# U's product in the low-rank mixer: six matmuls of 256 columns for two batches, twelve of 128 columns for the other two

## The chip, the cores and the metric

The kernel runs on one core of one Trainium2 chip. The metric is the device time of one execution in microseconds; the lower the better. The core has five engines that run beside each other, each with a queue of its own: TensorE (PE: matmuls, and PEld, the loads of their stationary operand), VectorE (DVE), ScalarE (ACT), GpSimd (POOL) and SyncE (SP, which issues the transfers here). Transfers run on 16 DMA engines.

## The reference

Two layers follow each other: a state-space layer (Mamba-2 in chunks) over 4 batches, 8 heads and 768 tokens, and a mixer with a low-rank product over the tokens and a two-layer network over the channels.

```
# state-space layer, per batch and head, in chunks of 32 tokens
M = (C @ B.T) * L;  y = M @ x + (C @ state) * decay;  state = decay * state + B.T @ x
# bridge: (B, H, S, D) -> x of (4, 768, 256)
xt = x.transpose(0, 2, 1)                 # (4, 256, 768)
h = xt @ U @ V                            # U (768, 32), V (32, 768)
u = x + h.transpose(0, 2, 1)
ch = np.maximum(u @ w_ch1, 0.0) @ w_ch2   # 256 -> 1024 -> 256
return u + ch
```

What the change touches is `xt @ U`: for each batch, 768 tokens are summed into 32 ranks for each of 256 channels.

## The kernel before

Tokens are taken in 6 blocks of 128 a batch (`NC`), channels in 2 halves of 128 (`NCB`). The state-space layer goes through 12 pairs of blocks, `k` = 0 to 11, three to a batch; its products are small ones in parts of the array: `gram` (L510), `state` (L545), `inter` (L630), `intra` (L655). `yout` copies its result to `yT` (channels by tokens) on ACT, and `ytokening` turns that on PE (L682) to `ytok` (tokens by channels). The transposes at L478 turn B and C.

The mixer of batch `b` follows. `project` is U's product (L712): the stationary operand is a block of U (128 tokens by 32 ranks), the moving operand the tokens of `ytok`, and the result goes into one of four quadrants of 32 partitions of one PSUM bank "w", so that each quadrant holds a part of the sum over the tokens. ACT copies the bank to `pT` (L717). `parted` adds the four quadrants with one product with a constant matrix (`spot`, L722) and copies the sum to `ps` (L724, and L725 on DVE). `added` multiplies by V (L732) and adds onto `yT` on DVE. The wide products of the two-layer network are all in `products` (L760), called by `plain`, `first`, `second` and `down`; `split` (L755) makes the parts of `u` on ACT and DVE for the batches that are computed in split form.

A matmul on plain 32-bit floats is two passes on PE: two weight loads and two matmuls, thus four instructions in PE's queue. One on the split form (`FP32R`), and a transpose, is one weight load and one matmul.

The order of work is written out by hand: `PLAN` is a list of words, and `follow` issues the steps in that order, so that each engine's queue is in the order of the list. `p0` to `p3` are U's product of the four batches, `q0` to `q3` the step `parted`, `a` the step `added`, `g`, `s`, `i`, `n`, `j` the small products of a pair, `m` and `M` the masks on DVE, `S` the split, `f`, `e`, `h`, `d` the network. Around the two words that matter here it reads:

```
... O2.1 X4 p0 P5 g3 m3 M3 q0 T5 T5 n3 a0.1 a0.0 ...
... U0.0.4 c8 p1 U0.1.4 c7 B8 q1 ...
```

In the twelve products of `project`, blocks are taken in pairs and each block in two halves of 128 channels; the quadrants come in the order 0, 1, 2, 3, 2, 3, 0, 1, 0, 1, 2, 3, so that each quadrant gets three products of 128 columns.

## Time and profile before

| | |
|---|---|
| median of 3 runs | 227.44 us (226.82 to 227.92) |
| the profiled execution | 227.39 us, of which the span from first to last instruction is 225.7 us |
| PE busy | 215.2 us (95%), 3048 matmul records |
| PEld busy | 183.0 us (81%), 3048 weight loads |
| DVE, ACT, POOL busy | 146.4, 107.9, 33.8 us |
| granted TensorE clock | full in all slices |
| transfers | 14.59 MB, of which 0.39 MB in 24 packets on the queue named "instruction" q8 |
| U's product (L712) | 96 records, starts at 27.9, 63.3, 136.8 and 169.1 us for the four batches |

The chain of waits is the chain of work that ended last, followed back from the last instruction; its pieces are given as start, length and what ran. "issue" is time in which an engine waited for nothing that the profile shows. A windows view gives, for a stretch of time, its length and then the busy time and the number of records for PE, PEld, DVE, ACT and POOL, the granted clock, the share of DMA time and the GB/s. Matmuls overlap, and their ends are modelled, so a busy PE is not PE at its peak.

### The profile page before, as it was taken

The page shows a single profiled execution, that of the slowest core. Times are in us where ns is not written, and L with a number is a line of the kernel's source. Part 1 is how long each engine was busy: PE and PEld are TensorE (multiplying, and loading weights), DVE is VectorE, ACT ScalarE, POOL GpSimd, SP SyncE. Part 2 cuts the span into 40 slices and gives each one's busy share as a digit, 9 for nine tenths or more (in the row PEclk, how much of TensorE's full clock was granted, in tenths as well). Part 3 has the DMA queues.
Part 4 walks back from the last instruction along what each step waited for, and adds up shares of the span by engine and source line. Part 5 has one row for each costly group of instructions (what it writes and reads, how often), then busy time and mean ns, then how long its engine had stood idle before and what let it go on. Part 6 is the DMA issues. An engine that isn't in the chain of part 4 may idle for free.

```text
span 225.7 us, 7080 instructions
## 1 busy us (share of the span) xinstructions
PE 215.2 (95%) x3048; PEld 183.0 (81%) x3048; DVE 146.4 (65%) x311; ACT 107.9 (48%) x250; POOL 33.8 (15%) x43
## 2 busy tenths in 40 slices
PE   7878999999999999999999999899999999999994
PEld 4645666676668889888899996697999999999993
DVE  4867779837853776667825837958925966484821
ACT  3334746476780363463226615376335655644610
POOL 3012301543824030304400000000000000000000
PEclk9999999999999999999999999999999999999999
DMA  5968989953873000631041301000010000001011
GB/s 79 129 119 143 191 131 182 214 130 98 186 95 73 23 27 3 95 69 49 7 61 56 49 25 49 6 0 3 0 49 0 25 3 23 24 25 46 1 49 46
DMA packets 69520, 14.59 MB, mean 65 GB/s; under 512 B 63792, under 2 KB 67696, under 8 KB 69488
## 3 DMA queue, kind: packets, MB, share of 16 engines
q1 hardware_dynamic: 69488, 14.13, 32.1%
q8 instruction: 24, 0.39, 0.7%
q14 instruction: 8, 0.07, 0.1%
HBM read 10.98 MB, written 3.15 MB: 63 GB/s over the span
## 4 chain that ended last, share of the span: by engine, by line
PE 80%; SPq 6%; DVE 6%; issue 2%; DMA 2%; ACT 1%; POOL 1%; DVEq 0%; POOLq 0%
PE x L760 29%; PE z L760 21%; PE y L760 12%; SPq L202 6%; PE y L655 4%; PE y L630 3%; DMA words<-in_moe_U_dram 2%; PE w L682 2%; DVE words L174 2%; PE w L712 2%; PE x L510 1%; PE w L545 1%; PE w L478 1%; PE z L510 1%; DVE M L174 1%
## 5 line engine op out<-in xcount | busy, mean ns | idle before, releaser
L760 PE MATMUL x<-u,w 128*128 128x384 f32 x144 | 32.8, 344 | 0.2 <-DVE M L174 0.2
L760 PE MATMUL z<-u,w 128*128 128x384 f32 x144 | 32.5, 341 | 0.0
L174 DVE SCALAR_TENSOR_TENSOR words<-words 128x768 fp32r<-128x768 f32 (+3 forms) x34 | 29.7, 873 | 1.6
L765 ACT ACTIVATE x<-x 128x384 f32<-128x384 f32 (+1 forms) x30 | 13.6, 454 | 29.8 <-PE x L760 29.8
L760 PEld LDWEIGHTS z<-u,w 128*128 128x128 f32 x144 | 24.9, 188 | 0.4 <-ACT z L765 0.2
L760 PEld LDWEIGHTS x<-u,w 128*128 128x128 f32 x144 | 24.4, 188 | 0.9 <-issue 0.3
L174 DVE SCALAR_TENSOR_TENSOR words<-x,words 128x384 fp32r<-128x384 f32 x24 | 13.2, 555 | 15.9 <-ACT words L794 14.1
L760 PE MATMUL x<-w2c,words 128*128 128x256 f32 x112 | 22.9, 341 | 0.0
L572 POOL TENSOR_TENSOR Sm<-S,own 128x256 f32<-128x256 f32 (+1 forms) x12 | 8.1, 674 | 85.2 <-DVE S L174 39.0
L760 PEld LDWEIGHTS x<-w2c,words 128*128 128x128 f32 x112 | 18.2, 189 | 1.6
L760 PE MATMUL y<-w,words 128*128 128x256 f32 x144 | 19.3, 282 | 0.0
L765 ACT ACTIVATE z<-z 128x384 f32<-128x384 f32 (+1 forms) x27 | 12.5, 465 | 13.7 <-PE z L760 11.1
L760 PEld LDWEIGHTS y<-w,words 128*128 128x128 f32 x144 | 18.7, 190 | 0.0
L174 DVE SCALAR_TENSOR_TENSOR words<-z,words 128x384 fp32r<-128x384 f32 x24 | 13.2, 551 | 5.4 <-ACT words L794 5.4
L794 ACT ACTIVATE words<-z 128x384 fp32r<-128x384 f32 x24 | 11.7, 492 | 9.9 <-PE z L760 9.7
L794 ACT ACTIVATE words<-x 128x384 fp32r<-128x384 f32 x24 | 11.6, 492 | 7.8 <-PE x L760 7.8
L655 PE MATMUL y<-M,x 64*32 64x64 f32 x768 | 12.6, 223 | 2.7 <-issue 1.6
L655 PEld LDWEIGHTS y<-M,x 64*32 64x32 f32 x768 | 8.1, 105 | 7.9 <-issue 3.9
L760 PE MATMUL x<-w,words 128*128 128x256 f32 x96 | 13.8, 286 | 0.0
L174 DVE TENSOR_TENSOR ytok<-x,ytok 128x256 f32<-128x256 f32 x10 | 4.2, 423 | 14.0 <-PE x L760 14.0
L174 DVE SCALAR_TENSOR_TENSOR S<-S,kept,w 128x64 f32<-128x64 f32 x40 | 11.2, 280 | 2.7 <-PE w L545 1.1
L760 PEld LDWEIGHTS x<-w,words 128*128 128x128 f32 x96 | 12.5, 190 | 0.3 <-issue 0.2
(148 smaller groups left out, 410.7 us busy)
## 6 DMA issues: line engine op xcount, KB each, us to landing
words<-in_moe_w_ch_dram SPq DMA_DIRECT2D x7, 512.0 KB, 5.0
x<-in_x_dram SPq DMA_DIRECT2D x24, 128.0 KB, 3.4
out_dram<-ytok SPq DMA_DIRECT2D x24, 128.0 KB, 1.7
bc<-in_B_dram SPq DMA_DIRECT2D x24, 64.0 KB, 3.1
bc<-in_C_dram SPq DMA_DIRECT2D x12, 128.0 KB, 3.1
words<-in_moe_w_ch_dram SPq DMA_DIRECT2D x2, 256.0 KB, 3.3
words<-in_moe_V_dram SPq DMA_DIRECT2D x4, 48.0 KB, 3.0
words<-in_moe_U_dram SPq DMA_DIRECT2D x1, 192.0 KB, 4.5
```

The costliest lines, as they stand in the source:

```text
L174: self.last = call(*args, **kwargs)
L202: op = issuer[0].dma_start(**kwargs)
L478: nc.tensor.transpose(out=tp[:, i, v], in_=s["BC"][:, i, c + v].rearrange("p h n -> p (h n)"), identity=ident)
L510: nc.tensor.matmul(out=g[r][cols, c], lhsT=s["T"][rows, 0, c, cols], rhs=s["Cm"][rows, :, :, ts(2 * c + p, Q)].rearrange("r v t i -> r v i ...
L572: nc.gpsimd.tensor_tensor(out=s["Sm"][:, sl], in0=s["S"][:, sl].rearrange("p i (s d) -> p i s d", s=2), in1=own2[:, b, 4 * q + sl.start:4 ...
L630: behind["first"].append(nc.tensor.matmul(out=y[r // 2][ts(r % 2, H), c, p], lhsT=own[ts(r, Q)], rhs=s["T"][ts(r, Q), 1, :, ts(2 * c + p, ...
L655: product = nc.tensor.matmul(out=y[n][ts(i, Q), c, p], lhsT=x_sb[k][half, c, h], rhs=s["M"][half, h // 2, c, h % 2], start=fresh(k, n, [i] ...
L682: nc.tensor.transpose(out=t[:, c, g], in_=yT[b][:, g, ts(2 * q + c, P)], identity=ident)
L712: nc.tensor.matmul(out=p[ts(to, Q), ts(half, P)], lhsT=U_sb[:, c + v], rhs=ytok[b][:, c + v, ts(half, P)], start=to not in seen, stop=True ...
L760: nc.tensor.matmul(out=t, lhsT=lhsT, rhs=rhs, start=start, stop=True, skip_group_check=True)
L765: nc.scalar.activation(t, t, AF.Copy, scale=1.0 + EPS)
L794: nc.scalar.activation(gs[j, m // 2][0][:, m % 2], t, AF.Relu, scale=NEAR)
```

## The change

For batches 0 and 1 U's product is issued as six matmuls, one a block of tokens, each over all 256 columns; block c goes to quadrant c mod 4, so that quadrants 0 and 1 get two products and quadrants 2 and 3 one. For batches 2 and 3 it stays as it was. `PLAN` and all else is the same.

```
         def project():
 
             p = bank("w", DM)
-            seen = set()
-            for c in range(0, NC, 2):
-                for half in range(NCB):
-                    for v in range(2):
-                        to = (c + 2 * half) % 4 + v
-                        nc.tensor.matmul(out=p[ts(to, Q), ts(half, P)], lhsT=U_sb[:, c + v],
-                                         rhs=ytok[b][:, c + v, ts(half, P)],
-                                         start=to not in seen, stop=True, skip_group_check=True)
-                        seen.add(to)
+            if b < 2:
+                for c in range(NC):
+                    nc.tensor.matmul(out=p[ts(c % 4, Q)], lhsT=U_sb[:, c], rhs=ytok[b][:, c],
+                                     start=c < 4, stop=True, skip_group_check=True)
+            else:
+                seen = set()
+                for c in range(0, NC, 2):
+                    for half in range(NCB):
+                        for v in range(2):
+                            to = (c + 2 * half) % 4 + v
+                            nc.tensor.matmul(out=p[ts(to, Q), ts(half, P)], lhsT=U_sb[:, c + v],
+                                             rhs=ytok[b][:, c + v, ts(half, P)],
+                                             start=to not in seen, stop=True, skip_group_check=True)
+                            seen.add(to)
             hold["p"] = pT = mix.tile([P, DM], FP32, tag="pT", name="pT", bufs=1)
             nc.scalar.copy(out=pT, in_=p)
```

## The prediction

> **What bounds the kernel now.** I read the page first (engines, clock, queues), then the chain of waits in order of time, then the waits of PE, then windows around the stops that these showed.

> ```profile
> span 225.7 us, 7080 instructions
> PE 215.2 (95%) x3048; PEld 183.0 (81%) x3048; DVE 146.4 (65%) x311; ACT 107.9 (48%) x250; POOL 33.8 (15%) x43
> PEclk9999999999999999999999999999999999999999
> q8 instruction: 24, 0.39, 0.7%
> PE 80%; SPq 6%; DVE 6%; issue 2%; DMA 2%; ACT 1%; POOL 1%; DVEq 0%; POOLq 0%
> ```

> PE (TensorE) is the bound: busy 95%, 80% of the chain, at the full granted clock. So a nanosecond taken from or given to PE's queue counts nearly whole, unless PE then waits for another engine. The q8 line matters later: 24 loads of instructions, 0.39 MB, so 16 KB each. PE and PEld have 6096 records; with 64 bytes for an instruction (my estimate: 0.39 MB over some 6150 PE instructions) one load is 256 instructions, and 24 x 256 = 6144 is about PE's whole program. I read q8 as PE's own instructions coming in while it runs.

> ```profile
> 27.94 1.27 PE w L712 x24
> ...
> 45.36 0.44 PE w L478 x4
> ...
> 56.73 0.12 PE x L510 x2
> 56.85 0.02 issue
> 56.87 0.34 PE z L510 x2
> ...
> 63.37 0.79 PE w L712 x24
> ...
> 65.65 0.43 PE w L722 x2
> ...
> 109.09 0.56 issue
> ...
> 143.94 0.37 PE y L655 x29
> 144.32 1.09 issue
> 145.41 0.30 PE y L655 x3
> ```

> These are pieces of the chain (start, length, what). U's product, L712, stands on it for batch 0 (27.94) and batch 1 (63.37), the two that the change touches. The two "issue" pieces are PE stops that wait for nothing the profile shows, and both fall inside a run of L655 products.

> ```profile
> L655 PE MATMUL y<-M,x 64*32 64x64 f32 x768 | 12.6, 223 | 2.7 <-issue 1.6
> ```

> The page's groups put 1.6 us of idle time before L655 down to "issue". How far apart are they in PE's own program? The windows view counts it (stretch, its length, busy time and count for each engine):

> ```profile
> 109.65:145.40 35.75, 34.49 (x510) 31.84 (x510) 22.56 (x46) 14.52 (x35) 1.44 (x2) 1.00 0.18 39
> 106.02:109.65 3.63, 3.07 (x129) 2.62 (x128) 1.94 (x5) 2.25 (x6) 1.85 (x2) 1.00 0.03 7
> 141.75:145.41 3.65, 2.57 (x145) 2.01 (x139) 3.51 (x9) 1.39 (x3) 0.51 (x1) 1.00 0.02 4
> 45.79:47.95 2.16, 2.16 (x134) 1.78 (x133) 0.38 (x2) 2.00 (x5) 0.09 (x1) 1.00 0.94 181
> ```

> ```profile
> q8 instruction: 1, 0.02, 5.3%
> q8 instruction: 1, 0.02, 5.1%
> q8 instruction: 1, 0.02, 4.6%
> q8 instruction: 1, 0.02, 5.2%
> ```

> (DMA view of 107.4 to 108.6, of 142.8 to 144.1, of 45.5 to 46.7, of 54.0 to 55.6.) The third belongs to row 4: a block of only 2.16 us without a counted stop, because its load began at 45.7, with the entry and not 1.2 to 1.5 us behind it: before it PE worked on long L760 products and its queue had read ahead.

> **The change, part by part.** The sum is made against the profiled execution, 227.39 us (span 225.7 and 1.7 around it); the median of the three runs is 227.44, the same for this purpose.

> (1) U's product itself, batches 0 and 1.

> ```profile
> L712 PEld LDWEIGHTS w<-ytok,UV x96: 106/110/110, 27.9 to 169.6; 128*32 128x32 f32 x96
> L712 PE MATMUL w<-ytok,UV x96: 272/273/297, 27.9 to 169.7; 128*32 128x128 f32 x96
> 63.30:64.17 0.87, 0.86 (x24) 0.59 (x24) 1.00 1.13 142
> ```

> A batch has 24 passes (12 matmuls, two passes each) of 273 ns that end within 0.86 us: four run side by side, one in each 32-column group of the array, in six rounds. A full-array pass of 128 columns takes 0.44/4 = 109 ns (L478), one of 256 columns 0.43/2 = 216 ns (L722). Before: every group gets six passes of 109, 654 ns in all. After: blocks 4 and 5 share groups 0 and 1 with blocks 0 and 1, so these get four passes of 216, 864 ns, and groups 2 and 3 two. PE's next work needs the whole array, so it waits for the longer pair: +0.21, less the first weight load's small part, 0.20 us. In batch 0 blocks 4 and 5 wait for the DVE copies of ytok, and end with two passes of 216 where one round of 109 ended before: +0.2 also. Ends: 0, were the idle groups used by the next work, and 1.7 us a batch, were wide passes not run side by side (12 x 216 less 864). I take 0.20 each, from the row that shows four groups at work: +0.40. The copy to pT, L722 and the mask chain move by the same 0.2; PE is full behind them, nothing covers it.

> (2) 24 instructions fewer in each of the two batches (six matmuls, two passes, a weight load and a matmul each). Every later block boundary falls 24, then 48, instructions later in the same program. Nothing else moves: all engines' orders, the DMAs and waits on SP and POOL are the same. What this does to each short block, by windows that begin 24 or 48 instructions later:

> ```profile
> 46.01:48.02 2.01, 2.01 (x139) 1.63 (x135) 0.45 (x3) 1.78 (x4) 0.15 (x1) 1.00 1.01 201
> 107.49:111.69 4.20, 3.64 (x139) 3.23 (x131) 3.60 (x10) 0.82 (x3) 1.59 (x2) 1.00 0.02 4
> 137.82:142.07 4.25, 4.14 (x141) 2.87 (x144) 3.07 (x9) 2.02 (x5) 0.00 (x0) 1.00 0.00 0
> 142.07:148.96 6.89, 5.80 (x149) 5.23 (x136) 4.91 (x11) 2.86 (x7) 0.51 (x1) 1.00 0.02 5
> ```

> - Stop at 144.32: its block now has 5.80 us of work, over 3.65: gone. L655's passes are recorded 223 ns long but follow each other 13 ns apart (29 in 0.37), so the loss was the gap between starts, the 1.09 and 0.2 that the end of the last pass covers, 1.3. What is late next is VectorE's mask, which frees the PSUM buffer of the third L760 product:

> ```profile
> 145.77 0.75 DVE L174 TENSOR_TENSOR M<-z,causal 128x256 int32<-128x256 int32 x2
> 147.36 0.72 PEld L760 LDWEIGHTS z<-u,w 128*128 128x128 f32 x4
> ```

>   The first of the two masks ends halfway, at some 146.15 to 146.2; that product's weights load at 147.36, so 1.16 can be had: -1.15 (ends 0 and -1.3).
> - Stop at 109.09: 0.56 and 0.2, so 0.77. The moved block has 3.64 us of work against 3.65, and ends among L760 products, where the queue has some depth: -0.65 (ends 0 and -0.77).
> - Slow piece at 56.87: 0.34 where neighbours take 0.12, and up to 0.4 by starts. Its load, entered for at 47.95, came as late as 54.2 (fourth q8 line) for a reason I do not see; the boundary falls some 0.2 to 0.4 later: -0.2 (ends -0.4 and +0.2).
> - A new stop at 48.0: the block is 2.01 us and its entry moves from the front of an L630 run to its middle, so less is read ahead. With the same load start the stop is nil, with none ahead 3.65 - 2.01 = 1.6. From how far the queue reads ahead in the traced block I take the third near the first end: +0.4 (ends -0.1 and +1.6).
> - The block of 137.82: 4.14 us of work, over 3.65: 0. All others are longer.

> Sum: 0.40 + 0.40 - 0.20 - 0.65 - 1.15 = -1.20, so 227.39 - 1.20 = 226.2 us.

> [...]

> **The rivals.**
> (a) The stops move and shrink as summed, new stop small: 226.2, its own range 225.4 to 227.0.
> (b) The stops at 109 and 144 are not a matter of position and stay (something not in the profile holds PE): only part (1) counts, 227.8. For it: the views name no releaser. Against: the exact 1024. [...]
> (c) The read-ahead at 46 is lost whole: the new stop is 1.6 and not 0.4: 227.4. For it: the entry at 45.79 now falls at 46.01, behind L630's first weight loads.
> (d) Slower: a load as late as that of the block entered at 47.95 strikes a short block. It began 6.2 us after the entry where the 23 others began at most 1.9 behind; on the block of 4.25 (137.82) that is 6.2 + 2.3 - 4.25, a stop of 4.3 and 230.5 us. 2.3 is what the two stops show from a packet's begin (107.5, 142.9) to the restart. It decides from a lateness of 4.3 us on: a stop of 2.3, the 1.2 gained and 1.1 more. For it: it happens once in 24 loads. Against: only four blocks are that short.

> **How the numbers follow.** (a) 0.48, (b) 0.17, (c) 0.22, (d) 0.13. About 0.5%, 1.1 us, is what a measurement of this kernel can tell from no change; the three runs span 226.82 to 227.92. The centre of (a) is just beyond that, and the dearer part of its range falls to "same", as (c) and (b) do for the most part. Faster 0.46, same 0.36, slower 0.18. The range that leaves 2 in 10 out: 225.2 (all stops gone, no new one) to 228.3 ((b), and the 0.5 that a run of before lay over its median).

> **What would show it.** L712's batches 0 and 1 as 12 longer passes, in batch 1 over 1.06 us instead of 0.86, batches 2 and 3 unchanged. The pieces 109 and 144 without "issue"; an "issue" piece near 48.5. Any stop left should lie a multiple of 256 instructions from the others, 48 further into the program than before. Wrong would be: stops at the same products as before (b), a stop over 1 us near 48 (c), or a stop of several us elsewhere (d).

## The result, and the profile after

The changed kernel took 225.84 us (median of seven executions, 225.44 to 226.65) against 227.56 us (seven, 226.82 to 228.46) for the kernel before: a ratio of 0.9927, 95% interval 0.9902 to 0.9952. That is faster by 0.7%, where the prediction took about 0.5% for what a measurement of this kernel can tell, and 0.4 us below the forecast of 226.2. In two later sets of ten executions, on two different chips, the same kernel had ratios of 0.9992 (0.9968 to 1.0016) and 0.9973 (0.9939 to 1.0008), which cannot be told from no change. Ratios here leave out the few executions that took over 1.5% longer than the fastest of their kernel. Why the gain went there is the larger part of what follows.

The page of the profiled execution (225.44 us), the lines that answer to those of before:

```profile
span 223.7 us, 7032 instructions
...
PE 214.8 (96%) x3024; PEld 182.1 (81%) x3024; DVE 146.7 (66%) x311; ACT 107.9 (48%) x250; POOL 33.8 (15%) x43
...
PEclk9999999999999999999999999999999999999999
...
q8 instruction: 24, 0.39, 0.8%
...
PE 88%; SPq 5%; DVE 3%; DMA 1%; issue 1%; ACT 1%
...
L655 PE MATMUL y<-M,x 64*32 64x64 f32 x768 | 12.0, 223 | 0.9 <-DVE settled L174 0.9
```

PE has 24 matmul records fewer (3048 before): there are twelve products fewer, and U's 48 products of before have 96 records, two each. PE is busy 0.4 us less in a span that is 2.0 us shorter. In the last line the group of L655 products has 0.9 us of idle time before it instead of 2.7, and "issue" no longer ends most of it. The chain of waits (start, length, what), at the places that the prediction spoke of:

```profile
27.75 1.47 PE w L709 x12
...
47.07 0.43 PE y L655 x31
...
47.80 0.47 PE y L655 x29
48.28 6.65 PE z L765 x20
...
56.92 0.74 DVE M L174 x2
57.66 1.52 DVE words L174
...
59.57 1.56 PE x L765 x4
...
63.29 0.99 PE w L709 x12
...
108.41 0.43 PE w L545 x29
109.22 1.62 PE z L765 x12
...
144.19 1.41 PE x L765 x8
145.59 0.89 PE z L765 x4
```

U's product is now L709 and its pieces are 1.47 and 0.99 us, against 1.27 and 0.79. The pieces of "issue" at 109 and 144 are gone, and there is none near 48. New is a stretch on VectorE from 56.92 to 59.57.

Both kernels issue PE's work in one order, so the start of each PE instruction can be compared between the two traces. The difference, after less before, moves in few steps: -0.19 at 21 us (in front of every change, so chance), +0.20 at batch 0's product, -0.15 by 56.3, -0.48 at 56.87, +0.54 at 59.6, +0.20 at batch 1's product, -0.83 at 109.65, -1.32 at 145.4, and about +0.1 at 147.4. They add up to -1.93; the two times differ by 1.95.

### The profile page after: what moved, and what is told of

It reads as the page before. It is cut to its first block, busy times and chain, and to the rows that moved or that the text cites. A ratio compares the mean times of both kernels' runs of the same rounds, so it can differ in the third digit from the quotient of the medians.

```text
span 223.7 us, 7032 instructions
## 1 busy us (share of the span) xinstructions
PE 214.8 (96%) x3024; PEld 182.1 (81%) x3024; DVE 146.7 (66%) x311; ACT 107.9 (48%) x250; POOL 33.8 (15%) x43
## 3 DMA queue, kind: packets, MB, share of 16 engines
HBM read 10.98 MB, written 3.15 MB: 63 GB/s over the span
## 4 chain that ended last, share of the span: by engine, by line
PE 88%; SPq 5%; DVE 3%; DMA 1%; issue 1%; ACT 1%
PE x L765 31%; PE z L765 23%; PE y L765 12%; SPq L202 5%; PE y L655 3%; PE y L630 3%; PE w L682 2%; PE x L510 2%; PE w L545 2%; DMA x<-in_x_dram 1%; PE w L478 1%; DVE M L174 1%; PE z L510 1%; PE w L709 1%; PE x L737 1%; PE w L136 1%
## 5 line engine op out<-in xcount | busy, mean ns | idle before, releaser
L765 PE MATMUL x<-u,w 128*128 128x384 f32 x144 | 32.8, 344 | 0.2 <-DVE M L174 0.2
L765 PE MATMUL z<-u,w 128*128 128x384 f32 x144 | 32.6, 342 | 0.0
L174 DVE SCALAR_TENSOR_TENSOR words<-words 128x768 fp32r<-128x768 f32 (+3 forms) x34 | 30.1, 887 | 1.6
L765 PEld LDWEIGHTS z<-u,w 128*128 128x128 f32 x144 | 24.9, 188 | 0.6 <-DVE M L174 0.2
L765 PEld LDWEIGHTS x<-u,w 128*128 128x128 f32 x144 | 24.4, 188 | 1.0 <-issue 0.3
L765 PE MATMUL x<-w2c,words 128*128 128x256 f32 x112 | 22.9, 341 | 0.0
L174 DVE SCALAR_TENSOR_TENSOR words<-x,words 128x384 fp32r<-128x384 f32 x24 | 13.1, 554 | 14.8 <-ACT words L799 12.9
L765 PEld LDWEIGHTS x<-w2c,words 128*128 128x128 f32 x112 | 18.2, 189 | 1.6
L765 PE MATMUL y<-w,words 128*128 128x256 f32 x144 | 19.3, 282 | 0.0
L770 ACT ACTIVATE z<-z 128x384 f32<-128x384 f32 (+1 forms) x27 | 12.5, 465 | 13.0 <-PE z L765 12.6
L765 PEld LDWEIGHTS y<-w,words 128*128 128x128 f32 x144 | 18.7, 190 | 0.0
L174 DVE SCALAR_TENSOR_TENSOR words<-z,words 128x384 fp32r<-128x384 f32 x24 | 13.2, 551 | 5.4 <-ACT words L799 5.4
L765 PE MATMUL x<-w,words 128*128 128x256 f32 x96 | 13.8, 286 | 0.0
L174 DVE SCALAR_TENSOR_TENSOR S<-S,kept,w 128x64 f32<-128x64 f32 x40 | 11.2, 279 | 2.8 <-PE w L545 1.2
L174 DVE TENSOR_TENSOR ytok<-x,ytok 128x256 f32<-128x256 f32 x10 | 4.2, 423 | 13.2 <-PE x L765 13.2
L655 PE MATMUL y<-M,x 64*32 64x64 f32 x768 | 12.0, 223 | 0.9 <-DVE settled L174 0.9
L765 PEld LDWEIGHTS x<-w,words 128*128 128x128 f32 x96 | 12.5, 190 | 0.3 <-issue 0.2
L655 PEld LDWEIGHTS y<-M,x 64*32 64x32 f32 x768 | 7.8, 105 | 5.8 <-DVE settled L174 1.9
```

The lines of the kernel that those rows point to most:

```text
L174: self.last = call(*args, **kwargs)
L655: product = nc.tensor.matmul(out=y[n][ts(i, Q), c, p], lhsT=x_sb[k][half, c, h], rhs=s["M"][half, h // 2, c, h % 2], start=fresh(k, n, [i] ...
L765: nc.tensor.matmul(out=t, lhsT=lhsT, rhs=rhs, start=start, stop=True, skip_group_check=True)
L770: nc.scalar.activation(t, t, AF.Copy, scale=1.0 + EPS)
```

## The experiments

Three questions. Are the stops a matter of position in PE's program, or does the wider product itself save something? What does each part alone do? And, once a later set of the changed kernel had shown no gain: what decides whether its gain stays?

A stop "between starts" is below the gap between the starts of two neighbouring PE instructions, "entry" is the start of the first instruction of a block of 256 (the size is the estimate of the prediction: 24 q8 loads, 0.39 MB, over some 6150 PE instructions). Counted as in the prediction, in every profile of this study each stop without a releaser that is named here as a stop at a boundary lies at instruction 194 modulo 256 of PE's program.

### The boundaries put back

```
-            p = bank("w", DM)
+            full = bank("w", 4 * P)
+            p = full[:, :DM]
...
                     nc.tensor.matmul(out=p[ts(c % 4, Q)], lhsT=U_sb[:, c], rhs=ytok[b][:, c],
                                      start=c < 4, stop=True, skip_group_check=True)
+                for c in range(NC):
+                    nc.tensor.matmul(out=full[ts(2 + c % 2, Q), DM:DM + 16], lhsT=U_sb[:, c],
+                                     rhs=ytok[b][:, c, :16], start=True, stop=True,
+                                     skip_group_check=True)
```

> The changed kernel with six more products in each of batches 0 and 1, sixteen columns wide, into a half of the bank of "w" that nobody reads; so U's product is six wide products there as in the changed kernel, but PE's program is again 24 instructions longer in each of the two batches, and every 256-instruction boundary falls where it fell before the change. Theory (the stops are a matter of position): "issue" pieces come back inside the L655 runs near 109 and 144, of 0.5 to 0.6 and 1.0 to 1.1 us, and the time is 227.4 to 228.2 us: 225.8, plus 1.3 and 0.8 for the two stops and up to 0.2 for the fillers, less 0.2 for the wait on VectorE's mask that falls away. Rival (the wider shape of the product, or its fewer products at that place, made the gain): no such pieces, 225.8 to 226.3 us.

Measured: 227.70 us, ratio to the kernel before 1.0014 (0.9985 to 1.0043). PE's timeline around the two places (start, length, what, count, idle time before):

```profile
109.75 0.42 PE L655 MATMUL y<-M,x 64*32 64x64 f32 x23
110.74 0.32 PE L655 MATMUL y<-M,x 64*32 64x64 f32 x9 [0.57 <-issue]
...
144.98 0.44 PE L655 MATMUL y<-M,x 64*32 64x64 f32 x29
146.50 0.30 PE L655 MATMUL y<-M,x 64*32 64x64 f32 x3 [1.07 <-issue]
```

The stops are back between the same products as before, x23 and x9, x29 and x3, at 0.57 and 1.07 us (0.56 and 1.09). The wide product is still in this kernel; what is gone is the shift. So the gain at these two places came from the shift. (The stops show that; the ratio alone would not, as the changed kernel itself had 0.9992 and 0.9973 later.)

### The boundaries moved 16 instructions the other way

```
-    warm(3, "x")
+    padded = bank("x", 4 * P)
+    idle(padded, 3)
+    for i in range(4):
+        nc.tensor.matmul(out=padded[ts(i % 4, Q), 3 * P:3 * P + 16], lhsT=ident[:, :Q],
+                         rhs=ident[:, :16], start=True, stop=True, skip_group_check=True)
```

> The kernel before with 4 sixteen-column products at the very start, read by nobody: 16 instructions, 8 of them matmuls. Theory (position): both "issue" pieces stay, but 8 L655 matmuls earlier in their runs: x29 before and x3 behind the stop near 144 become x21 and x11, x23 and x9 near 109 become x15 and x17; the time is 227.2 to 227.9 us. Rival (the stops belong to a product or to a wait that the views do not show): x29 and x3, x23 and x9 as before.

Measured: 227.82 us in one execution. PE's timeline:

```profile
110.10 0.34 PE L659 MATMUL y<-M,x 64*32 64x64 f32 x15
110.75 0.35 PE L659 MATMUL y<-M,x 64*32 64x64 f32 x17 [0.31 <-issue]
...
145.04 0.41 PE L659 MATMUL y<-M,x 64*32 64x64 f32 x21
145.80 0.33 PE L659 MATMUL y<-M,x 64*32 64x64 f32 x11 [0.34 <-issue]
```

(L659 is L655 here.) Both stops moved by exactly eight matmuls, x15 and x17, x21 and x11. With the run above this shows that position in PE's program set the place of these two stops; a product or a hidden wait would not move with four products at 3 us. The sizes are smaller, 0.31 and 0.34 us where they were 0.56 and 1.09, and a third stop of 0.79 us between starts appeared one block earlier, at 106.2: the count gave the place here, but not the size.

### The shift of the change, with the product of before

The same edit with `range(52)`: 208 instructions, which is 256 less 48.

> The kernel before, U's product in twelve products for all batches, with 52 sixteen-column products at the very start, where PE only waits for its first data; nobody reads them. That is 208 instructions, 256 less 48, so that from batch 1 on every boundary falls at the same work as in the changed kernel. Theory (position): no "issue" pieces at 109 and 144, the narrower product of batches 0 and 1 is kept, and the time is 225.4 to 225.9 us, at or below the changed kernel. Two theories differ on the early boundaries, which fall 48 instead of 0 or 24 instructions later there: if none of them is short enough, nothing is lost. Rival (shape of the product): the stops stay and the time is 227.4 to 228.

Measured: ratio 1.0006 (0.9969 to 1.0043), some 227.7 us, so the time of the rival, but not its mechanism. The stops at 109 and 144 are gone with the product of before in place: in the comparison of starts with the kernel before, PE wins 0.77 at the one and 1.30 at the other, as the theory of position has it. As much was lost elsewhere; the chain shows another stop:

```profile
57.74 0.62 PE y L634 x25
...
59.26 1.55 issue
60.81 0.41 PE y L659 x19
```

The load for the block that begins at 60.81 began only at 58.41, 6.7 us after the entry into the one before. Near 50 PE lost another 0.5, and it was 1.0 to 1.5 us late already between 16 and 28 us, part of which is the padding at the start. The forecast looked at the early boundaries by the length of their blocks alone, and that was not enough.

### The change for batch 0 alone, and for batch 1 alone

```
-            if b < 2:
+            if b < 1:
```

> The change for batch 0 alone: six products of 256 columns there, twelve of 128 columns for batches 1, 2 and 3; the shift is 24 instructions from batch 0 on. Theory (position): nothing near 144 (that block then has 4.8 us of work); the block entered at 107.3 has only 2.3 us of work (3.08 by the trace of before, less the stop of 0.8 in it), so a stop of up to 1.3 us falls 24 instructions later than before's, among the L760 products near 110.4, or a smaller one so far as the queue has read ahead; 226.0 to 227.2 us. Rival (each changed batch brings its own share of the gain by its shape): half the gain, 226.6 to 226.8, and the stop of before at the same L655 products near 109 or 144.

Measured: 227.42 us, ratio 0.9987 (0.9965 to 1.0009), above the 226.0 to 227.2 that were expected. The chain:

```profile
48.80 1.12 issue
...
50.23 6.65 PE z L765 x20
...
111.00 0.55 PE z L765 x3
111.56 0.56 issue
112.12 1.23 PE z L765 x9
```

The stop of 109 has moved into the L760 products (L765 here), 24 instructions on, as expected, and takes 0.56 (0.84 between its two starts, where 0.12 is usual); nothing is left at 144. Not expected was the first line: a stop of 1.12 at 48, which the first profile of the changed kernel did not have, though up to there the two programs are the same.

```
-            if b < 2:
+            if b == 1:
```

> The change for batch 1 alone: twelve products for batch 0, so the boundaries up to 63 us lie where they lay before the change, and 24 instructions later behind it. Theory (position): no stop at 48, as in both profiles with that position; the stop of 0.56 (0.72 by starts) near 111 that the run with batch 0 alone showed; none at 144; so 227.5 less 1.3 for the stop at 144, plus 0.2 for the mask behind it and 0.2 for the wide product: 226.3 to 226.9 us. Rival (the stop at 48 has nothing to do with batch 0's part): it is there too, and 227.4 to 228.2.

Measured: 226.98 us, ratio 0.9965 (0.9928 to 1.0002), 0.1 above what was expected. There is no stop at 48 and none at 144. At 111 only 0.2 us is lost, where batch 0 alone lost 0.7 at the same place in the program; the load began 0.12 us after the entry here (108.46) and 0.65 there (109.73). At 57.8 PE loses 0.8 against the first profile of the changed kernel, of which 0.5 is made up by 60.6: another late load (55.43, 6.9 us after the entry).

### The wide product for all four batches

```
-            if b < 2:
+            if b < 4:
```

> The wide product in six for all four batches: boundaries up to 136 us as in the changed kernel, 72 instead of 48 instructions later than before behind batch 2's product, 96 behind batch 3's. Theory (position): the blocks behind 136 stay above 3.65 us of work, no stop appears, and the two wider products cost up to 0.2 us each: 225.9 to 226.3 us. Rival (each wide product brings 0.85 by its shape, half of what the two of the change brought): 224.0 to 224.4.

Measured: 227.08 us, ratio 0.9975 (0.9956 to 0.9994), on the chip on which the changed kernel has 227.58. The number expected was wrong because its base was; the rival's 224 is out. In the profile nothing is lost at 109 and 144, batch 2's product sets PE back 0.19 us against the changed kernel, made up 0.7 us further on, and batch 3's 0.20, which stays; and there is again a piece of "issue" of 0.85 at 48.77. The wide product itself took 0.2 us longer in each of the four batches (0.20 in batches 0 and 1 of the changed kernel, 0.19 and 0.20 in 2 and 3 here); behind batch 2 that cost nothing in the end.

### The changed kernel twice more

> The changed kernel once more, for a second profile and ten more times. Theory: whether a stop stands near 48 us hangs on how early that block's load begins, which differs from one execution to the next (45.64 us in the first profile of this kernel, and no stop; 0.71 us behind the entry in the run with batch 0 alone, where all of PE's work up to there is the same, and a stop of 1.12 us). Then most of the ten times lie at 225.4 to 226.7, some may lie 1.3 above, and a profile that shows a piece of issue there is one of these. No stop at 109 or 144 in any case. Rival (the first seven times were a lucky set, the change does nothing): median 227.0 to 227.6.

Measured: 227.58 us (225.89 to 228.36), ratio 0.9992: the time of the rival. The chain of this profile:

```profile
48.38 0.41 PE y L655 x25
48.79 1.12 issue
...
50.22 6.65 PE z L765 x20
...
57.47 0.62 PE y L630 x25
...
58.90 0.49 issue
59.39 0.46 PE y L655 x31
```

> The changed kernel a third time, beside the other three on one chip. Its first profile has no stop at 48 us and 225.44; its second has one of 1.12 us (1.33 by starts) and another 0.5 us gone at 59, and its ten times have a median of 227.58. Theory (a stop at 48 that some executions have and others not, by when that block's load begins): the profile shows either the load 0.1 us before the L630 run's start or earlier and no stop, with 225.4 to 226.6, or the load 0.8 to 1.0 behind it and a stop of 0.85 to 1.15, with 227.0 to 228.0; nothing between. Rival (some other thing on the second chip made it slow, and the stop is part of every execution): the stop is there whatever the time.

Measured: 227.31 us (226.05 to 228.41), ratio 0.9973, with pieces of "issue" of 0.53 at 48.78 and 1.04 at 58.29. The load began 0.60 us behind the start of the L630 run, so there is something between the two cases after all, and the expected gap was wrong. Against the first profile of this kernel the second is 0.57 us late when it comes to 46 us, loses 1.33 at 48 and 0.72 at 59, of which 0.56 is made up by 61.7, and from there to the end stays 2.1 behind within 0.15. In the third it is 0.56, 0.78, 1.27 and 0.56. So the whole difference lies before 62 us, and 1.5 of it at 48 and 59.

Of these 20 executions four lie below 226.7; of the first seven all did. The program is the same in all three profiles, and one of them has no stop at 48; so it differs from one execution to the next.

### A product in eight, balanced over the quadrants

```
-                for c in range(NC):
-                    nc.tensor.matmul(out=p[ts(c % 4, Q)], lhsT=U_sb[:, c], rhs=ytok[b][:, c],
-                                     start=c < 4, stop=True, skip_group_check=True)
+                for c in range(4):
+                    nc.tensor.matmul(out=p[ts(c, Q)], lhsT=U_sb[:, c], rhs=ytok[b][:, c],
+                                     start=True, stop=True, skip_group_check=True)
+                for c in range(4, NC):
+                    for half in range(NCB):
+                        nc.tensor.matmul(out=p[ts(2 * half + c - 4, Q), ts(half, P)], lhsT=U_sb[:, c],
+                                         rhs=ytok[b][:, c, ts(half, P)],
+                                         start=False, stop=True, skip_group_check=True)
```

For all four batches the same eight products stand in place of the twelve everywhere.

> U's product of batches 0 and 1 in eight: blocks 0 to 3 over 256 columns, one in each quadrant, blocks 4 and 5 in two halves of 128, one half in each quadrant, so that every quadrant has the same 654 ns of passes as before the change; 16 instructions fewer a batch, boundaries 16 and 32 later. Theory (position): the product costs 0.2 less a batch than the six; the block that ended at 144 has over 4 us of work and no stop; the block entered at 107.35 has 2.7 us of work against 3.65 and shows a stop of 0 to 0.9 us near 110.8, by how far the queue reads ahead there: 225.4 to 226.8 us. Rival (shape): the stops of before stay, 227.4 to 227.9.

> The product in eight for all four batches: as with batches 0 and 1 alone up to 136 us, then boundaries 48 instructions later than before, as in the changed kernel, and 64 behind batch 3's product. Theory: the time of the run with batches 0 and 1 alone within 0.3 us, no stop near 144. Rival (fewer products, by shape): 0.5 or more below that run.

> The product in eight for all four batches once more, on another chip and beside the changed kernel. Theory: its boundary near 48 lies only 16 instructions later than before the change, its load begins some 0.2 us behind the start of the L630 run, so there is a loss of 0.3 us at most there, and none at 109 and 144: 225.6 to 226.5 us whatever the changed kernel does on that chip. Rival (the first run of it was lucky as the first of the changed kernel was): 227.0 to 227.7.

Measured: for batches 0 and 1 226.75 us (ratio 0.9973, 0.9941 to 1.0004), and the ten times lie in two heaps, five from 225.64 to 226.03 and five from 227.48 to 228.28. For all four batches 226.27 (0.9941, 0.9904 to 0.9977) on the same chip, and 227.62 (0.9972, 0.9930 to 1.0015) on another, so the forecast that this one would hold whatever the changed kernel does has failed. The first two profiles have no "issue" at 48, 109 or 144; the third has one of 1.06 at 49.36 and one of 0.64 at 59.25, and its load near 46 us began 0.84 us behind the start of the L630 run, where that of the same program began 0.21 behind in the run before. One position, two outcomes: position alone does not decide the stop at 48. The product itself is as cheap as the twelve: in the chain of the first of these profiles batch 1's takes 0.58 us for the eight passes of 256 columns and 0.22 for the eight of 128, 0.80 in all, against 0.79 for the twelve products and 0.99 for the six.

### The small packets taken away from the load

At the time of the load near 46 us, B and C of pair 7 come in as packets of 64 and 128 bytes. One word of the plan moves them:

```
-    'T6 u4 T6 B7 i4 g5 c4 c4 n4 w6 s5 j4 y4 R1 M5 U0.0.7 ...
+    'T6 u4 T6 i4 g5 c4 c4 n4 w6 s5 j4 y4 R1 M5 B7 U0.0.7 ...
```

> The changed kernel with one word of the plan moved: B7, the load of B and C for pair 7, is issued behind M5 (near 49 us) instead of behind u4 (near 43 us), and so behind the weights of w6 in SP's queue. PE's and VectorE's orders are the same, and so are all boundaries. It takes the some 3000 packets of 64 and 128 bytes that run from 44 to 47 us away from the time at which the block entered at 46 asks for the next. Theory A (the load waits behind those packets): it begins within 0.3 us of the start of the L630 run, no stop at 48, and 225.4 to 226.6 us, with up to 0.7 more if pair 7 then comes late to VectorE near 53. Theory B (the load is late because the boundary lies 24 instructions further, past the point to which the queue had read ahead): it still begins 0.8 to 1.0 behind in most executions, the stop is 0.85 to 1.15, and the time is 227.0 to 228.0.

Measured: 226.32 us (225.52 to 227.26), ratio 0.9927 (0.9897 to 0.9958), on the chip on which the changed kernel has 227.31 and 0.9973. The chain of its profile at 48:

```profile
47.60 0.62 PE y L630 x25
...
48.86 0.43 PE y L655 x31
...
49.59 0.45 PE y L655 x32
50.04 6.65 PE z L765 x20
```

No stop, and the whole chain holds no piece of "issue" of 0.5 us or more. The DMA view (packets in the window; then by queue: packets, MB, share of 16 engines) for the second profile of the changed kernel, 46.2 to 47.1 and 47.1 to 47.2:

```profile
DMA packets 1679, 0.17 MB, mean 189 GB/s; under 512 B 1679, under 2 KB 1679, under 8 KB 1679
...
q1 hardware_dynamic: 1679, 0.17, 141.7%
...
q8 instruction: 1, 0.02, 66.6%
```

and for the kernel with B7 late, 46.8 to 47.4, and 50.6 to 50.7:

```profile
DMA packets 1, 0.02 MB, mean 27 GB/s; under 512 B 0, under 2 KB 0, under 8 KB 0
...
q8 instruction: 1, 0.02, 11.2%
...
q8 instruction: 1, 0.02, 74.4%
```

The first weights of the L630 run load at 46.31 in the first of these and at 47.53 in the second. PE's own work runs alike in both: from its last wait ahead of that run (a semaphore at 43.95 and at 45.17) to these weights pass 2.36 us, as in all six profiles with this shift. What differs is the transfers. With 1679 small packets in the 0.9 us from just ahead of that start, the load begins only at 47.16, 0.85 behind it; with no other packet from 45.75 on it begins at 46.88, 0.65 ahead of it, which is earlier than expected. So with the boundary at the same place the load could begin early; that something among the transfers made it late is my reading of the pair. In the late case 2082 packets moved between 46.04 and 47.15, all of them under 512 bytes, and the load still did not begin; so in that stretch only small packets moved ahead of it. One thing more differs: PE ran 1.2 us later in the run with B7 late, so that the weights of w5 (packets of 2048 bytes, issued ahead of B7) had passed as well. This run does not separate the two fully.

The number of small packets does not tell how late a load is. In the first profile of the changed kernel 1462 of them stand in the 0.9 us up to the load's begin, and it was 0.10 ahead of the run. There they had begun to come in 1.75 us ahead of the run, in the second profile 0.5.

The times go the same way: the ten are lower than the ten of the changed kernel on this chip in 81 of the 100 pairs. The profiled execution is the slowest of its ten, 227.26, because PE is 1.8 us late already at 22 us; from there to the end it stays 1.8 us behind the first profile of the changed kernel, within 0.1. The next load (last line) begins 0.9 us after its entry, and nothing is lost at 59.

The load near 46 us and the stop behind it, over all profiles but the one with 52 products, where the boundary lies in other work; times of the load are from the first weight load of the L630 run, the stop is that between starts:

| kernel | instructions later than before | load begins | stop |
|---|---|---|---|
| four products at the start | -16 | -0.73 | 0 |
| before | 0 | -0.01 | 0 |
| boundaries put back | 0 | -0.44 | 0 |
| batch 1 alone | 0 | -0.20 | 0 |
| eight, two batches | 16 | +0.26 | 0.25 |
| eight, all; again | 16 | +0.21; +0.84 | 0.26; 1.27 |
| changed, first; third; second | 24 | -0.10; +0.60; +0.85 | 0; 0.74; 1.33 |
| six for all; batch 0 alone | 24 | +0.92; +0.98 | 1.07; 1.33 |
| changed, B7 late | 24 | -0.65 | 0 |

In these rows the loads that began 0.01 to 0.73 ahead have no stop, the two 0.21 and 0.26 behind have 0.26 and 0.25, the one 0.60 behind has 0.74, and the four 0.84 to 0.98 behind have 1.07 to 1.33. Whether the boundary's place matters here as well stays open: none of the four profiles with a shift of 0 or -16 has a stop, but three of them had the small packets early, as the first profile of the changed kernel had.

## Why the prediction was right, and where it was not

**(1) The product, +0.20 a batch.** Right: 1.47 against 1.27 and 0.99 against 0.79 in the chain, +0.20 each in the comparison of starts, and 0.2 again in batches 2 and 3 with six for all. The working, that quadrants 0 and 1 get four passes of 216 ns where each had six of 109, is borne out by the balanced eight, which takes the 0.2 back (0.80).

**(2) The stop at 144, -1.15.** Right in mechanism and close in size: -1.32, so the whole 1.3 went. What was to be late next, VectorE's mask, shows in PE's waits as it was named:

```profile
PE x L765 <- DVE M L174: 0.4, 2, 0.2
```

That is two waits of 0.2 at most; the third L760 product loaded its weights 0.19 us later than the rest had gained, about 0.1 of which stayed. Net -1.22, and the term was 0.07 off.

**The stop at 109, -0.65.** Right in mechanism: -0.83, the whole stop, since its load began at 107.30, 0.27 ahead of the entry. With 24 instructions instead of 48 a stop was left, of 0.7 us in batch 0 alone, where the load began 0.65 us after the entry, and 0.2 in batch 1 alone, where it began 0.12 after.

**The slow piece at 56.87, -0.2.** The step failed. PE won 0.48 there and lost 0.54 at 59.6: the chain goes over to VectorE, masks and weight words from 56.92 to 59.57, and PE's next product waits for them. The term looked for what is late next only at 144; here VectorE had no slack. Net +0.06.

**The new stop at 48, +0.4 (ends -0.1 and +1.6).** The step failed in its cause. Its value in the profile on record is 0, in two others 0.74 and 1.33, all inside the ends. But I put it down to how far PE's queue reads ahead behind a boundary that lies 24 instructions further. The run with B7 late has that same boundary, a load 0.65 us ahead of the run's start, and no stop, so the cause that I gave is what failed. How far the queue had read ahead was my estimate. What the traces show is where loads begin: behind wide L760 products up to about 1.0 us ahead of the entry (165.52 for 166.51 in the kernel before), and at this place 0.85 us behind the run's start with 1679 small packets in the 0.9 us up to the load, 0.65 ahead of it with no other packet. That the load waited for other transfers is my reading of these two. So the term is not one number but differs between executions, and rival (c), 227.4, which took the stop at its whole size, is within 0.2 us of the medians 227.58 and 227.31 of the later sets, whose profiles also lose a net 0.2 and 0.7 near 59. The range of 225.2 to 228.3 held all three medians; its lower end was that no such stop comes, its upper end came from rival (b).

**Rival (b), the stops are not a matter of position, 227.8.** Out: they went with the shift, came back with it, and moved by eight matmuls for 16 instructions.

**Rival (d), a late load strikes.** It did not happen in the profile on record, but it exists, and not only in short blocks: the load of the block entered near 48 to 50 (52 with 52 products at the start) began 6 to 8 us after the entry in 11 of 14 profiles, and behind most of these PE then stopped near 59: "issue" 0.49 and 1.04 in the later profiles of the changed kernel, 1.55 with 52 products at the start. It was priced as 4.3 us on one of the four shortest blocks; it cost up to 1.55 behind a block of 9 us, and in the later profiles of the changed kernel 0.56 of that was made up within 2.5 us.

So the sum of -1.20 was met by -1.93 in the profile on record: the stops at 109 and 144 gave 0.25 more than forecast, there was none at 48 (0.4 more), 0.19 and 0.15 came in small pieces that no term names, and 56.87 gave 0.26 less. In the later profiles the stops at 48 and 59 took 1.5 of it back. That the median on record came within 0.4 us of the forecast is therefore in part luck: the later medians lie 1.4 and 1.1 us above 226.2, and "faster" holds in one set of three.

**How many boundaries cost something.** In the profile of the kernel before, PE's program has 24 places at instruction 194 modulo 256. At 21 of them the starts of neighbouring PE instructions, weight loads among them, lie at most 0.21 us apart; the other three are the piece at 56.87 and the stops at 109 and 144 (0.31, 0.77 and 1.31). In the first profile of the changed kernel they lie at most 0.26 us apart at all 24. In the second profile of the eight for all four the chain has "issue" of 1.06 at 49.36 and of 0.64 at 59.25. So few of the boundaries cost time here, and these few decide the case.

## What to carry to other kernels

An "issue" piece inside a run of tiny PE products is worth counting. The two here stood 1024 instructions apart in PE's program; 16 instructions added at its start moved both by eight matmuls, and 48 taken out ahead of them won 0.83 and 1.32 us, which has nothing to do with what the edit computes. Whether such pieces of another kernel stand a multiple of 256 apart, and move in the same way, is a thing to count and to try there. Before moving a boundary into or out of a dense stretch, look at the transfers around the time of its load: here 1679 small packets in 0.9 us went with a load 0.85 us behind, and no other packet with one 0.65 ahead. With one transfer moved away the changed kernel had 0.9927, where on the same chip it had 0.9973 without that, and nine of ten executions below 227.1 us instead of three; the two intervals just overlap. A kernel with B7 late and the balanced eight, which does not pay the 0.2 a batch of the six, was not run. And a gain that rests on when a load comes in has to be measured in more than one set: 0.9927, 0.9973 and 0.9992 are the same kernel.

## What the runs showed of the hardware that was not expected

- The q8 load near 46 us began 0.85 us behind the start of the L630 run with 1679 packets of under 512 bytes in 0.9 us, and 0.65 ahead of it with none. But with 1462 of them, begun earlier against PE's work, it was 0.10 ahead.
- From the begin of such a load to the first instruction of its block, where PE waited for it, mostly passed 2.2 to 2.8 us (107.48 to 109.65 in the kernel before, 47.16 to 49.91 in the second profile of the changed one). It was 3.0 at the extra stop with four products at the start (103.23 to 106.21), and 3.8 in the run with B7 late (17.18 to 20.96), where the one packet of the load took 2.5 us.
- The load of the block entered near 48 to 50 us (52 with 52 products at the start) began 6 to 8 us after the entry in 11 of 14 profiles, though no data packet moves for 3.3 to 5.5 us of that: 54.33 in the first profile of the changed kernel, 6.4 us after the entry. With the boundaries put back, with four products at the start and with B7 late it began 0.9 to 1.9 us after the entry. What holds it is open; no run told it apart.
- Why the transfers lie differently against PE's work from one execution to the next is open as well. In the first and second profile of the changed kernel SyncE's queue shows the weights of w5 issued in 1.90 and 3.15 us:

```profile
39.77 1.90 SPq L202 DMA_DIRECT2D words<-in_moe_w_ch_dram  x1
42.95 0.37 SPq L202 DMA_DIRECT2D bc<-in_B_dram  x1
```

```profile
40.35 3.15 SPq L202 DMA_DIRECT2D words<-in_moe_w_ch_dram  x1
43.59 0.42 SPq L202 DMA_DIRECT2D bc<-in_B_dram  x1
```

  B7 (the second line of each) is issued 2.8 and 2.7 us ahead of the L630 run, so at nearly the same point of PE's work. But the large packets of w5 end 1.5 us ahead of that run in the first and 0.3 us in the second, and the packets of B7, which follow them, begin 1.75 and 0.5 us ahead of it.
- PE reached 21 us up to 1.8 us later in some executions of the same order of work, 0.4 to 1.6 of it at the boundary near 20 us (1.6 in the run with B7 late, by the load named above). That alone is as large as the change.
